# A scan with two feed-forward layers: weights of layer 2 prepared over 30 groups instead of 24, and a scheduler that lets fewer operations compete

## The chip, the cores and the metric

One core of a Trainium2 chip runs the kernel. The metric is the device time of one execution in microseconds (us), the median of several executions. The core has TensorE (PE), which multiplies, VectorE (DVE), ScalarE (ACT) and GpSimd (POOL), which work on elements, and SyncE (SP), from whose queue all transfers of this kernel are issued.

## The reference

```python
S, D, d_ff = 6080, 256, 2048                 # all in float32
sig = 1 / (1 + exp(-f_logit));  f = lower_bound + (1 - lower_bound) * sig
for t in range(S):
    h = f[:, t] * h + (1 - f[:, t]) * x[:, t];  y[:, t] = h       # gated scan
g = y @ w1_in;  y1 = maximum(0.01 * g, g) @ w1_out                # layer 1
g = y1 @ w2_in; out = where(g > 0, g, exp(minimum(g, 0)) - 1) @ w2_out   # layer 2
```

## The kernel before

**Tiles.** The 6080 tokens are cut into 12 chunks: eleven of 512, and chunk 1 of 448. The hidden width of 2048 is cut into four groups `q`, so a layer is 48 groups and the kernel is 96, in the order of a list `stream`: first chunks 0 and 1 by turns, then chunks 2 to 11 of layer 1, then layer 2 from group 48 (`turn2`). The output of layer 1 goes to DRAM (`y1d`, L989) and is fetched again in layer 2 (L605).

**Products.** A float32 product is made of three matmuls in a rounded format (`mm3`): L617 takes the high parts of weight and operand, L618 the low part of the operand, L619 the low part of the weight. So an operand is usable for L617 once ACT has cast its high part (L496 for the scan's rows of chunks 0 and 1, L459 for the sums of later chunks, L797 and L920 for the hidden values), and for L618 once DVE has subtracted (L498, L461, L801, L923). Most products are done with seven multiplications in place of eight, with sums on DVE (L455, L668, L908) and snapshots of a PSUM bank on ACT (L665 into `sn`). L691, L718 and L723 are the activation of layer 1; L728, L732, L738 and L743 on ACT and L734, L740 and L745 on DVE that of layer 2.

**Scan.** `gated` does for each half of the features a tanh and a scaling on ACT (L570, L573), a product on DVE (L577) and the scan (L585); for chunks 0 and 1 PE transposes the inputs (L547), later DVE does (L567).

**Weights.** `weights` makes high and low parts of one unit (`wI0` to `wI7` of the first matrix, `wO0` to `wO3` and `wE0` to `wE3` of the second). A unit is two loads (L337), work on DVE (L365, L374, L378, L392), on POOL (L368) and on ACT (L371, L390). The units of layer 2 also get their sums (L279, ten of the sixteen units) and are stored in DRAM (L399, L401) while layer 1 still uses the weight tiles; `reload` fetches them (L414) when layer 2 begins.

**What sets the order.** Nothing is issued where it stands in the code. Every operation is added to a `Plan` with an engine, a cost, predecessors, buffers that it takes and gives, and a due time. `Plan.emit(near)` (L49) then builds all queues: of the open operations of an engine those that could begin within `near` us of the earliest possible beginning are candidates, and the one with the earliest due time (`rank`) is issued. The costs are the planner's own. Each engine works through its queue in that order; a buffer goes to whoever is issued first.

The sixteen units of layer 2 are called at groups 16, 17, 19, 20, 22, 23, 25, 26, 28, 29, 31, 32, 34, 35, 37 and 38; a unit's due time lies 20 us behind the beginning of its group, and its loads wait for the first product of two groups earlier. `SEVEN` says which groups use seven multiplications for the second matrix as well.

Of the kernel before, what the change touches and what calls it, by code (L numbers as in the profile page):

```python
# [9 lines left out]
F32 = mybir.dt.float32  # L10
# [6 lines left out]
P = 128  # L17
# [95 lines left out]
def kernel(  # L113
# [30 lines left out]
    NQ = NP // 2  # L144
# [10 lines left out]
    NC = len(sizes)  # L155
# [9 lines left out]


    SI, SO = 7 * P, 2 * D
    SEVEN = {1: (1, 2), 2: (0, 1)}

    def sums(l, u):  # L170

        return u[0] == "I" or u[0] == "O" and u[1] in SEVEN[l]

    def stored(u):

        return SO if not sums(2, u) else SI if u[0] == "I" else 8 * P

    units = [("I", z) for z in range(NP)] + [(r, z) for z in range(NQ) for r in "OE"]
    size = {u: SO if u[0] == "E" or u[0] == "O" and not any(u[1] in v for v in SEVEN.values()) else SI for u in units}
    w = {u: const.tile([P, 2 * size[u]], F32R, name=f"w{u[0]}{u[1]}") for u in units}  # L180
    w2d = {u: dram.tile([P, 2 * stored(u)], F32, name=f"w2d{u[0]}{u[1]}") for u in units}
    y1d = [dram.tile([D, n], F32, name=f"y1d{c}") for c, n in enumerate(sizes)]
# [37 lines left out]
    DMA, LATE, FAR, SGN = 0.475, 2.3, 4.5, 0.8  # L220
# [13 lines left out]
    def dma(*a, **k):  # L234
        return plan.add("SP", *a, **k)
# [16 lines left out]

    def seven(l, c, q):

        return q in SEVEN[l] and not (l == 1 and c < 3) and not (l == 2 and c == NC - 1)

    due_in = [0.0]
    for l, c, q in stream:
# [147 lines left out]
    def reload(u, after):  # L406

        q = u[1] // 2 if u[0] == "I" else u[1]
        m = stored(u)

        def load(to, at, n):
            def run():
                dst, src = (t.rearrange("p (j m) -> p j m", j=2) for t in (w[u].bitcast(F32), w2d[u]))
                nc.sync.dma_start(out=dst[:, :, to * P : (to + n) * P], in_=src[:, :, at * P : (at + n) * P])  # L414

            return run

        due = due_in[first[2, "w", q]] + (-12.0 if u[0] == "I" else 0.0)
        parts = [(0, 0, m // P)] if m < 8 * P else [(0, 7, 1), (1, 1, 6)]
        ready = wdone[2, u] + after  # L420
        wdone[2, u] = [dma(2 * part[2] * P / 590.0, due, load(*part), ready, late=LATE) for part in parts]

        def back(after):

            wdone[2, u] = [dma(0.5, due_in[-1 - NQ] - 3.0, load(0, 0, 1), after, late=LATE)]

        return back

# [53 lines left out]
    def rows(c, filled, take, read=()):  # L482

        n = sizes[c]
        xb = {"rows": {}}
        bt = take

        def part(j, k):
            return xb["p"][2][:, 4 * HC * j + k * n : 4 * HC * j + (k + 1) * n]

        last = []
        for k in range(KD):
            def word(k=k):
                return bt["bt"][2][:, k * n : (k + 1) * n]

            hi = act(s1(n), None, lambda k=k, word=word: nc.scalar.copy(out=part(0, k), in_=word()), [filled[k]] + last,  # L496
                     take=[(xb, "p", "op")] if k == 0 else [])
            lo = dve(v1(n), None, lambda k=k, word=word: nc.vector.tensor_tensor(  # L498
                out=part(1, k), in0=word(), in1=part(0, k).bitcast(F32), op=ALU.subtract), [hi])
            last.append(lo)  # L500
            xb["rows"][k] = [lo]
        free([*last, *read], [(bt, "bt", bt["pool"])])
        xb["row"] = lambda k: (part(0, k), part(1, k))
        return xb
# [95 lines left out]
    def fetched(c, gates, hold):  # L600
        n = sizes[c]
        bt = {"pool": "bt"}
        filled = []
        for k in range(KD):
            filled.append(dma(DMA, None, lambda k=k: nc.sync.dma_start(  # L605
                out=bt["bt"][2][:, k * n : (k + 1) * n], in_=y1d[c][k * P : (k + 1) * P, :],
            ), gates + yd[c] + filled[:1], take=[(bt, "bt", "bt")] if k == 0 else [], late=LATE))
        ys[c] = operands(c, filled, bt, (), hold)


# [15 lines left out]
    def group(i):  # L626
# [7 lines left out]
        final = i == len(stream) - 1  # L634
        wi = [o for p in pairs for o in wdone.get((l, ("I", p)), ())]
        wo = {r: wdone.get((l, (r, q)), ()) for r in "OE"}
        if l == 1 and c < 3:
            wo["O"] = wplain.get((l, ("O", q))) or wo["O"]
        count = [0]

# [377 lines left out]

    later = [u for q in range(NQ) for u in (("I", 2 * q), ("I", 2 * q + 1), ("O", q), ("E", q))]
    begin2 = 16  # L1020
    gap = (turn2 - 8 - begin2) / len(later)
    spread = {}
    for z, unit in enumerate(later):
        spread.setdefault(begin2 + int(z * gap), []).append(unit)
# [3 lines left out]
    for i, (l, c, q) in enumerate(stream):  # L1028
        back = [firsts[i - 6] if i >= 6 else None]
        if q == 0:  # L1030
            hold = firsts[i - 1 : i - 1 + 1] if i > 4 else []
            if l == 1:
                gated(c, c < 2, back + ([firsts[i - 4]] if i >= 4 else []), hold)
            else:
                fetched(c, back, hold)
# [6 lines left out]
        if l == 2 and c == 0:  # L1042
            for u in mine:
                backs[u] = reload(u, [last_use[q][u[0] != "I"]])
        if l == 2 and c == NC - 1 and q in SEVEN[2]:
            backs["O", q]([last_use[q][1]])
        at = len(prods)
        o = group(i)
        if l == 1 and c in (1, 2):
            for z in ([q - 1] if q else []) + ([q] if q == NQ - 1 else []):  # L1050
                for u in (("I", 2 * z), ("I", 2 * z + 1)) if c == 1 else (("O", z),):
                    if sums(1, u):
                        finish(u, [prods[-1], outs[-1]])
        firsts.append(prods[at])
        if l == 1 or c == NC - 2:
            last_use[q] = (prods[-1], o)
    plan.emit(0.1)


# [28 lines left out]
```

## Time and profile before

| | |
|---|---|
| median of 3 executions | 994.54 us (994.28 to 1003.21) |
| profiled execution | 995.75 us |
| its span on the core | 993.9 us |
| granted TensorE clock, mean | 0.998 of full speed |
| PE busy | 982.4 us, 99% |
| DVE busy | 878.9 us, 88% |
| ACT busy | 774.5 us, 78% |
| POOL busy | 37.8 us, 4% |

The time of the profiled execution is 1.85 us more than its span, which is what lies around the span. Busy time is counted by instruction; an instruction that waits in front of an engine is not busy. A row of the timeline gives the start, the length, the engine, the line of the kernel, the operation, the tile written and the tiles read, and in brackets the idle time of the engine just before it with what ended it.

### The profile page before, as it was taken

To read this page: it belongs to the slowest core of one execution; us is meant where nothing else is said; L and a number is where in the kernel's file an instruction comes from. 1 tells how busy PE (TensorE), PEld (TensorE's weight loads), DVE (VectorE), ACT (ScalarE), POOL (GpSimd) and SP (SyncE) were. 2 spreads that over 40 slices of the span, in tenths; PEclk is the share of its full clock that TensorE was granted. 3 is DMA by queue.
4 is the path that set the end of the run, shared out by engine and by line. 5 is a ranking of instruction groups with operands and counts; after the bars stand their busy time and mean duration, and the time that the engine had idled before them with its cause. 6 is when DMAs were issued, how large, how long until landed. Compare 5 with 4: busy or idle time off the path is not lost.

```text
span 993.9 us, 20119 instructions
## 1 busy us (share of the span) xinstructions
PE 982.4 (99%) x8234; PEld 969.8 (98%) x8234; DVE 878.9 (88%) x1356; ACT 774.5 (78%) x1139; POOL 37.8 (4%) x38
## 2 busy tenths in 40 slices
PE   7999999999999999999999999999999999999998
PEld 6999999999999999999999999999999999999998
DVE  7899989999999999886678888988988989889875
ACT  6777787887878878867687878788877888788864
POOL 1122000100000010100000000000000000000000
PEclk9999999999999999999999999999999999999999
DMA  6542304435254443302760101101111021010110
GB/s 185 138 115 56 82 12 115 119 97 155 80 150 142 108 138 112 85 23 95 260 226 22 22 22 41 22 23 22 31 35 22 23 44 22 22 23 22 32 22 22
DMA packets 159853, 74.36 MB, mean 75 GB/s; under 512 B 133520, under 2 KB 147600, under 8 KB 159760
## 3 DMA queue, kind: packets, MB, share of 16 engines
q1 hardware_dynamic: 159760, 73.08, 27.4%
q8 instruction: 64, 1.05, 0.4%
q14 instruction: 29, 0.24, 0.1%
HBM read 48.01 MB, written 25.03 MB: 73 GB/s over the span
## 4 chain that ended last, share of the span: by engine, by line
PE 94%; DVE 4%; POOL 1%; issue 1%; DMA 0%; ACT 0%; DVEq 0%; SPq 0%
PE bank L617 28%; PE bank L618 28%; PE bank L619 28%; PE bank L843 2%; PE seed L619 2%; PE seed L618 2%; PE seed L617 2%; POOL ws L368 1%; DVE ws L378 0%; DVE op L801 0%; DVE ws L374 0%; DVE h L279 0%; DVE bt L585 0%; DMA raw<-in_f_logit_dram 0%; DVE up L365 0%
## 5 line engine op out<-in xcount | busy, mean ns | idle before, releaser
L617 PE MATMUL bank<-op,wI 128*128 128x256 f32 (+2 forms) x1136 | 318.1, 280 | 0.8 <-ACT sn L665 0.6
L618 PE MATMUL bank<-op,wI 128*128 128x256 f32 (+2 forms) x1136 | 317.3, 279 | 1.4 <-DVE op L498 1.4
L619 PE MATMUL bank<-op,wI 128*128 128x256 f32 (+2 forms) x1136 | 316.9, 279 | 0.0
L617 PEld LDWEIGHTS bank<-op,wI 128*128 128x128 f32 x1136 | 213.6, 188 | 3.7 <-ACT sn L665 0.9
L618 PEld LDWEIGHTS bank<-op,wI 128*128 128x128 f32 x1136 | 213.5, 188 | 3.6 <-DVE op L498 2.1
L619 PEld LDWEIGHTS bank<-op,wI 128*128 128x128 f32 x1136 | 213.5, 188 | 0.4
L618 PE MATMUL bank<-op,wE 128*128 128x256 f32 (+2 forms) x662 | 190.9, 288 | 0.0
L617 PE MATMUL bank<-op,wE 128*128 128x256 f32 (+2 forms) x662 | 190.8, 288 | 0.0
L619 PE MATMUL bank<-op,wE 128*128 128x256 f32 (+2 forms) x662 | 190.7, 288 | 0.0
L618 PE MATMUL bank<-op,wO 128*128 128x256 f32 (+2 forms) x672 | 187.7, 279 | 0.0
L617 PE MATMUL bank<-op,wO 128*128 128x256 f32 (+2 forms) x672 | 187.7, 279 | 0.0
L619 PE MATMUL bank<-op,wO 128*128 128x256 f32 (+2 forms) x672 | 187.6, 279 | 0.0
L668 DVE TENSOR_TENSOR h<-bank,sn 128x512 f32<-128x512 f32 (+1 forms) x176 | 120.1, 682 | 36.3 <-PE bank L619 30.0
L617 PEld LDWEIGHTS bank<-op,wO 128*128 128x128 f32 x672 | 126.3, 188 | 0.4
L619 PEld LDWEIGHTS bank<-op,wE 128*128 128x128 f32 x662 | 124.3, 188 | 2.3
L619 PEld LDWEIGHTS bank<-op,wO 128*128 128x128 f32 x672 | 126.2, 188 | 0.3
L618 PEld LDWEIGHTS bank<-op,wO 128*128 128x128 f32 x672 | 126.2, 188 | 0.3
L665 ACT COPY sn<-bank 128x512 f32<-128x512 f32 (+1 forms) x176 | 102.6, 583 | 30.0 <-PE bank L619 28.3
L617 PEld LDWEIGHTS bank<-op,wE 128*128 128x128 f32 x662 | 124.5, 188 | 1.3
L618 PEld LDWEIGHTS bank<-op,wE 128*128 128x128 f32 x662 | 124.3, 188 | 1.2
L801 DVE TENSOR_TENSOR op<-h,op 128x1024 fp32r<-128x1024 f32 (+1 forms) x78 | 95.6, 1226 | 8.9 <-ACT op L797 8.4
L801 DVE TENSOR_TENSOR op<-ws,op 128x1024 fp32r<-128x1024 f32 (+1 forms) x72 | 86.1, 1209 | 15.1 <-ACT op L797 15.1
(112 smaller groups left out, 1770.5 us busy)
## 6 DMA issues: line engine op xcount, KB each, us to landing
ws<-in_moe_w_in_dram SPq DMA_DIRECT2D x32, 255.6 KB, 3.7
ws<-in_moe_w_out_dram SPq DMA_DIRECT2D x32, 255.6 KB, 3.3
w2dI<-ws SPq DMA_DIRECT2D x16, 448.0 KB, 3.0
wI<-w2dI SPq DMA_DIRECT2D x8, 896.0 KB, 5.8
y1d<-t SPq DMA_DIRECT2D x22, 256.0 KB, 2.0
bt<-y1d SPq DMA_DIRECT2D x22, 256.0 KB, 2.8
raw<-in_f_logit_dram SPq DMA_DIRECT2D x80, 64.0 KB, 3.0
raw<-in_x_dram SPq DMA_DIRECT2D x80, 64.0 KB, 2.5
```

The source lines that it names most:

```text
L368: sg = pool(SGN, None, lambda: nc.gpsimd.tensor_scalar(out=fr(), in0=top().bitcast(I8), scalar1=2.0, scalar2=-2.0, op0=ALU.min, op1=ALU.ma ...
L617: nc.tensor.matmul(ps[:, s], wop[0], a[0][:, s], start=start and z == 0, stop=False, skip_group_check=True)
L618: nc.tensor.matmul(ps[:, s], wop[0], a[1][:, s], start=False, stop=False, skip_group_check=True)
L619: nc.tensor.matmul(ps[:, s], wop[1], a[0][:, s], start=False, stop=stop, skip_group_check=True)
L665: return act(s1(2 * h), None, lambda: nc.scalar.copy(out=ps(name), in_=ps("X")), after, take=[(b, name, "sn")])
L668: return dve(v1(2 * h), None, lambda: nc.vector.tensor_tensor(out=half(name, s), in0=two(ps(bank)), in1=two(ps(sn)), op=ALU.add), after, **k)
L801: gates[name] = dve(v1(2 * n), None, lambda name=name, g=g: nc.vector.tensor_tensor(out=gate(name, 1), in0=whole(g), in1=gate(name, 0).bit ...
L843: nc.tensor.matmul(dst, ops(part, j, t), wide(z, j), start=s in fresh and t % 2 + j + z == 0, stop=False, skip_group_check=True)
```

## The change

Three things differ that can alter what is issued. The rest of the diff is written otherwise with the same meaning: `SEVEN` becomes a table from layer and group to a range of chunks with the same members, two casts of a type to itself are added, and `hold` and `last_use` are formed otherwise.

1. The stretch over which the units are called ends 2 groups ahead of layer 2 instead of 8. The gap between units is 30/16 = 1.875 groups instead of 24/16 = 1.5, and they are called at groups 16, 17, 19, 21, 23, 25, 27, 29, 31, 32, 34, 36, 38, 40, 42 and 44.
2. `near` is 0.05 us instead of 0.1, for the whole program.
3. The due time of the small reload of `wO1`'s first 128 columns ahead of the last chunk is that of its own group instead of that of the chunk's first group.

```diff
@@ SEVEN
-    SEVEN = {1: (1, 2), 2: (0, 1)}
+    SEVEN = {(1, 1): range(3, 12), (1, 2): range(3, 12), (2, 0): range(0, 11), (2, 1): range(0, 11)}
@@ reload
-        def back(after):
+        def back(i, after):
 
-            wdone[2, u] = [dma(0.5, due_in[-1 - NQ] - 3.0, load(0, 0, 1), after, late=LATE)]
+            wdone[2, u] = [dma(0.5, due_in[i] - 3.0, load(0, 0, 1), after, late=LATE)]
@@ calls
     begin2 = 16
-    gap = (turn2 - 8 - begin2) / len(later)
+    gap = (turn2 - 2 - begin2) / len(later)
...
-            hold = firsts[i - 1 : i - 1 + 1] if i > 4 else []
+            hold = firsts[-1:] if i > 4 else []
...
-        if l == 2 and c == NC - 1 and q in SEVEN[2]:
-            backs["O", q]([last_use[q][1]])
+        if l == 2 and c and c - 1 in SEVEN.get((2, q), ()) and c not in SEVEN[2, q]:
+            backs["O", q](i, [last_use[q][1]])
...
-        if l == 1 or c == NC - 2:
-            last_use[q] = (prods[-1], o)
-    plan.emit(0.1)
+        last_use[q] = (prods[-1], o)
+    plan.emit(0.05)
```

Both programs hold the same instructions on every engine; what differs is their order and which buffer each uses. In three places the order is shown.

At the start, on DVE, from the last two steps of the first weight units to the operands of chunk 1 (`op0`, `op1` are the scan's outputs as operands, `t0` its inputs, `bank3` and `bank5` PE's transposes). Before:

```order
L378 TENSOR_TENSOR ws0_134<-ws0_134 128x512
L392 TENSOR_TENSOR wI0_63<-ws2_136,wI0_63 128x512
L577 SCALAR_TENSOR_TENSOR t0_143<-t2_145,bank3_118 128x512
L392 TENSOR_TENSOR wI1_64<-ws0_134,wI1_64 128x512
L585 SCALAR_TENSOR_TENSOR bt0_129<-t2_145,t0_143 128x512
L365 TENSOR_SCALAR up0_146<-ws1_135 128x512
L498 TENSOR_TENSOR op0_122<-bt0_129,op0_122 128x512
L374 SCALAR_TENSOR_TENSOR ws0_134<-ws1_135,ws0_134 128x512
L577 SCALAR_TENSOR_TENSOR t0_143<-t1_144,bank5_120 128x448
L378 TENSOR_TENSOR ws0_134<-ws0_134 128x512
L585 SCALAR_TENSOR_TENSOR bt0_129<-t1_144,last_h_110,t0_143 128x448
```

And now:

```order
L577 SCALAR_TENSOR_TENSOR t0_143<-t2_145,bank3_118 128x512
L378 TENSOR_TENSOR ws0_134<-ws0_134 128x512
L392 TENSOR_TENSOR wI0_63<-ws2_136,wI0_63 128x512
L585 SCALAR_TENSOR_TENSOR bt0_129<-t2_145,t0_143 128x512
L392 TENSOR_TENSOR wI1_64<-ws0_134,wI1_64 128x512
L498 TENSOR_TENSOR op0_122<-bt0_129,op0_122 128x512
L365 TENSOR_SCALAR up0_146<-ws1_135 128x512
L577 SCALAR_TENSOR_TENSOR t0_143<-t1_144,bank5_120 128x448
L374 SCALAR_TENSOR_TENSOR ws0_134<-ws1_135,ws0_134 128x512
L585 SCALAR_TENSOR_TENSOR bt0_129<-t1_144,last_h_110,t0_143 128x448
L378 TENSOR_TENSOR ws0_134<-ws0_134 128x512
```

The scan's steps L577, L585 and L498 moved ahead of steps of the weights, and L378 of `wO0` moved behind the second scan. On ACT beside it, from the cast of `wO0` to the cast of the first hidden values (`op2`), as a piece of the difference:

```order
+L496 CAST op_123<-bt_129 128x448
+L691 ACTIVATE h_130<-seed_114 128x512
 L390 CAST wO_71<-ws_134 128x512
-L691 ACTIVATE h_130<-seed_114 128x512
-L496 CAST op_123<-bt_129 128x448
+L570 ACTIVATE t_145<-bank_117 128x448
 L797 CAST op_124<-h_130 128x1024
-L570 ACTIVATE t_145<-bank_117 128x448
```

L390 moved behind L496 and L691, and L570 of the next half moved ahead of L797. On ACT some 100 us into the program, at the first products of chunk 2 (`sn1` is the snapshot that frees the bank for the next product), before:

```order
L665 COPY sn0_137<-bank3_118 128x512
L570 ACTIVATE t2_145<-t2_145 128x512
L718 ACTIVATE h0_130<-seed0_114 128x2x256
L573 ACTIVATE t2_145<-t2_145,fb_109,fa_108 128x512
L570 ACTIVATE t0_143<-t0_143 128x512
L665 COPY sn1_138<-bank3_118 128x512
```

And now:

```order
L665 COPY sn0_137<-bank4_119 128x512
L570 ACTIVATE t2_145<-t2_145 128x512
L718 ACTIVATE h0_130<-seed0_114 128x2x256
L573 ACTIVATE t2_145<-t2_145,fb_109,fa_108 128x512
L665 COPY sn1_138<-bank4_119 128x512
L570 ACTIVATE t0_143<-t0_143 128x512
```

The second L665 passed one L570. On DVE in a chunk of layer 2 (the one at 610 us), at the change from one chunk's operands to the next, before:

```order
L801 TENSOR_TENSOR op4_126<-ws2_136,op4_126 128x1024
L461 TENSOR_TENSOR op6_128<-bt0_129,op6_128 128x768
L461 TENSOR_TENSOR op2_124<-bt0_129,op2_124 128x768
L745 SCALAR_TENSOR_TENSOR ws1_135<-ws1_135,h2_132 128x1024
L668 TENSOR_TENSOR h1_131<-bank0_115,sn1_138 128x2x256
L461 TENSOR_TENSOR op2_124<-bt0_129,op2_124 128x256
L801 TENSOR_TENSOR op0_122<-ws1_135,op0_122 128x1024
```

And now:

```order
L801 TENSOR_TENSOR op1_123<-ws1_135,op1_123 128x1024
L461 TENSOR_TENSOR op6_128<-bt0_129,op6_128 128x768
L745 SCALAR_TENSOR_TENSOR ws2_136<-ws2_136,h2_132 128x1024
L461 TENSOR_TENSOR op2_124<-bt0_129,op2_124 128x768
L801 TENSOR_TENSOR op0_122<-ws2_136,op0_122 128x1024
L668 TENSOR_TENSOR h0_130<-bank3_118,sn1_138 128x2x256
L461 TENSOR_TENSOR op2_124<-bt0_129,op2_124 128x256
```

L745 passed the second L461, and L801 of `op0` passed L668. The same move of L745 is made in nine more chunks.

On SP the last unit's two stores (L399, L401 of `w2dE3`) moved from ahead of chunk 9's outputs (L989) to the two refetches of the first chunk of layer 2 (L605): the queue now reads L399, L605, L401, L605, and then the first reload L414 of `wI0`. The small reload of change 3 has kept its place. At the start the load of chunk 1's last inputs (L538) passed one half of a load of weights (L337).

## Rows read from the trace of the kernel before

**Rows 1.** The page: busy time by engine, and the chain that ended last.

```profile
PE 982.4 (99%) x8234; PEld 969.8 (98%) x8234; DVE 878.9 (88%) x1356; ACT 774.5 (78%) x1139; POOL 37.8 (4%) x38
...
PE 94%; DVE 4%; POOL 1%; issue 1%; DMA 0%; ACT 0%; DVEq 0%; SPq 0%
```

**Rows 2.** Waits of PE: waiting line and releaser, total us, times, longest.

```profile
PE bank L618 <- DVE op L498: 1.4, 3, 0.6
PE bank L617 <- ACT sn L665: 0.6, 1, 0.6
PE seed L619 <- DVE wI L392: 0.3, 1, 0.3
PE bank L617 <- ACT op L496: 0.2, 1, 0.2
```

**Rows 3.** Busy time by stretch, with instruction counts, then granted clock, DMA share.

```profile
7.20:10.60 3.40, 1.61 (x12) 1.23 (x10) 3.37 (x5) 0.97 (x2) 0.64 (x2) 1.00 1.01 303
10.60:14.10 3.50, 2.87 (x14) 2.87 (x15) 3.40 (x6) 2.89 (x7) 1.02 (x1) 0.52 0.37 78
...
160.00:400.00 240.00, 240.00 (x2071) 237.99 (x2071) 230.91 (x375) 198.20 (x299) 15.29 (x15) 1.00 0.44 121
400.00:485.00 85.00, 85.00 (x733) 84.19 (x732) 63.91 (x94) 61.34 (x91) 0.55 (x1) 1.00 0.29 94
...
560.00:950.00 390.00, 390.00 (x3325) 386.63 (x3324) 354.58 (x519) 315.60 (x438) 0.00 (x0) 1.00 0.13 27
```

**Rows 4.** Timeline of PE: the late matmuls, and two that are merely longer.

```profile
23.07 0.47 PE L618 MATMUL bank<-op,wI 128*128 128x448 f32 x1 [0.60 <-DVE op L498]
...
28.88 0.47 PE L618 MATMUL bank<-op,wI 128*128 128x448 f32 x1 [0.37 <-DVE op L498]
...
101.24 0.38 PE L617 MATMUL bank<-op,wI 128*128 128x256 f32 x1 [0.55 <-ACT sn L665]
...
212.60 0.38 PE L618 MATMUL bank<-op,wE 128*128 128x256 f32 x1
...
395.18 0.38 PE L617 MATMUL bank<-op,wI 128*128 128x256 f32 x1
```

**Rows 5.** Timeline of DVE: start-up, then the beginning and one chunk of layer 2.

```profile
19.38 0.69 DVE L378 TENSOR_TENSOR ws<-ws 128x512 f32<-128x512 f32 x1
...
22.94 1.21 DVE L801 TENSOR_TENSOR op<-h,op 128x1024 fp32r<-128x1024 f32 x1
...
28.21 0.61 DVE L498 TENSOR_TENSOR op<-bt,op 128x448 fp32r<-128x448 f32 x1
...
491.14 0.95 DVE L461 TENSOR_TENSOR op<-bt,op 128x768 fp32r<-128x768 f32 x1
...
612.88 1.23 DVE L745 SCALAR_TENSOR_TENSOR ws<-ws,h 128x1024 f32<-128x1024 f32 x1
```

**Rows 6.** Timeline of ACT: start-up, and the snapshot at 100 us.

```profile
22.78 0.55 ACT L570 ACTIVATE t<-bank 128x448 f32<-128x448 f32 x1
...
100.09 0.62 ACT L570 ACTIVATE t<-t 128x512 f32<-128x512 f32 x1
100.61 0.57 ACT L665 COPY sn<-bank 128x512 f32<-128x512 f32 x1
```

**Rows 7.** DVE from 160 to 485 us by line: busy us, mean ns, idle before.

```profile
L392 DVE TENSOR_TENSOR ws<-ws,ws 128x896 f32<-128x896 f32 (+2 forms) x16 | 15.2, 952 | 0.9 <-ACT ws L390 0.7
...
L378 DVE TENSOR_TENSOR ws<-ws 128x512 f32<-128x512 f32 x16 | 10.9, 681 | 0.6 <-ACT ws L371 0.2
L374 DVE SCALAR_TENSOR_TENSOR ws<-ws,ws 128x512 int32<-128x512 int32 x16 | 10.8, 672 | 0.0
L279 DVE TENSOR_TENSOR ws<-ws 128x128 f32<-128x128 f32 x40 | 9.8, 283 | 0.1
```

**Rows 8.** Timeline of SP's queue: the last unit's last store, the first refetch.

```profile
409.27 0.34 SPq L401 DMA_DIRECT2D w2dE<-ws  x1
...
456.09 0.88 SPq L605 DMA_DIRECT2D bt<-y1d  x2
```

More of the change, by code (lines that the diff above doesn't have):

```diff
@@ L167 @@
     SI, SO = 7 * P, 2 * D
-    SEVEN = {1: (1, 2), 2: (0, 1)}
+    SEVEN = {(1, 1): range(3, 12), (1, 2): range(3, 12), (2, 0): range(0, 11), (2, 1): range(0, 11)}
     def sums(l, u):
-        return u[0] == "I" or u[0] == "O" and u[1] in SEVEN[l]
+        return u[0] == "I" or u[0] == "O" and len(SEVEN.get((l, u[1]), ())) > 0
     def stored(u):
@@ L178 @@
     units = [("I", z) for z in range(NP)] + [(r, z) for z in range(NQ) for r in "OE"]
-    size = {u: SO if u[0] == "E" or u[0] == "O" and not any(u[1] in v for v in SEVEN.values()) else SI for u in units}
+    size = {u: SO if u[0] == "E" or not (sums(1, u) or sums(2, u)) else SI for u in units}
     w = {u: const.tile([P, 2 * size[u]], F32R, name=f"w{u[0]}{u[1]}") for u in units}
@@ L253, in seven @@
     def seven(l, c, q):
-        return q in SEVEN[l] and not (l == 1 and c < 3) and not (l == 2 and c == NC - 1)
+        return c in SEVEN.get((l, q), ())
     due_in = [0.0]
@@ L605, in fetched @@
             filled.append(dma(DMA, None, lambda k=k: nc.sync.dma_start(
-                out=bt["bt"][2][:, k * n : (k + 1) * n], in_=y1d[c][k * P : (k + 1) * P, :],
-            ), gates + yd[c] + filled[:1], take=[(bt, "bt", "bt")] if k == 0 else [], late=LATE))
+                out=bt["bt"][2].bitcast(F32)[:, k * n : (k + 1) * n], in_=y1d[c][k * P : (k + 1) * P, :],
+            ), gates + yd[c] + filled[:1], take=[(bt, "bt", bt["pool"])] if k == 0 else [], late=LATE))
         ys[c] = operands(c, filled, bt, (), hold)
@@ L636, in group @@
         wo = {r: wdone.get((l, (r, q)), ()) for r in "OE"}
-        if l == 1 and c < 3:
+        if l == 1 and c < min(SEVEN.get((1, q)) or [NC]):
             wo["O"] = wplain.get((l, ("O", q))) or wo["O"]
@@ L1044 @@
                 backs[u] = reload(u, [last_use[q][u[0] != "I"]])
-        if l == 2 and c == NC - 1 and q in SEVEN[2]:
-            backs["O", q]([last_use[q][1]])
+        if l == 2 and c and c - 1 in SEVEN.get((2, q), ()) and c not in SEVEN[2, q]:
+            backs["O", q](i, [last_use[q][1]])
         at = len(prods)
         o = group(i)
-        if l == 1 and c in (1, 2):
+        if l == 1 and c:
             for z in ([q - 1] if q else []) + ([q] if q == NQ - 1 else []):
                 for u in (("I", 2 * z), ("I", 2 * z + 1)) if c == 1 else (("O", z),):
-                    if sums(1, u):
+                    if sums(1, u) and (u[0] == "I" or c == min(SEVEN[1, z]) - 1):
                         finish(u, [prods[-1], outs[-1]])
         firsts.append(prods[at])
-        if l == 1 or c == NC - 2:
-            last_use[q] = (prods[-1], o)
-    plan.emit(0.1)
+        last_use[q] = (prods[-1], o)
+    plan.emit(0.05)
 _INS = ["x", "f_logit", "lower_bound", "moe_w_in", "moe_w_out", "moe2_w_in", "moe2_w_out"]
```

2 lines of the change are left out of this document (1 added, 1 removed).

## The prediction, made before the changed kernel was run

> **What bounds the kernel now.** The first view to read is the page: PE is busy 982.4 us, 99% of the span, and the chain that ended last is PE for 94% [rows 1]. DVE with 88% comes next. So the time is PE's work, which the change leaves alone matmul by matmul, plus the places where PE stands still. Those are the second view, PE's waits [rows 2]. Leaving out the first loads and the identity, which the change doesn't touch, they are 1.4 + 0.6 + 0.3 + 0.2 = 2.5 us in six places, none after 101.24 [rows 4]. The third view, busy time by stretch, says it for the places at which the change is aimed: from 160 to 400 us PE is busy 240.00 of 240.00 us, from 400 to 485 it is 85.00 of 85.00, and from 560 to 950 it is 390.00 of 390 [rows 3]. DVE is nearly full in the first of them, 230.91 of 240 or 96%, has room in the second, 63.91 of 85 or 75%, and 91% in the third. Whatever is moved from the first to the second is moved out from under a PE that didn't wait for it. The reader is to see that a full second engine is not yet a bound: what counts is idle time of PE, and there is next to none.
>
> **The longer stretch.** A unit costs DVE, by its four largest lines, (15.2 + 10.9 + 10.8 + 9.8) / 16 = 2.9 us [rows 7]. At one unit in 1.5 groups of some 10 us that is about 19% of DVE, at one in 1.875 groups about 16%. From 160 to 400 us DVE would so fall from 96% to some 93%, and the share after 400 would rise from 75% by about five units of 2.9 us, 14.5 of 85 us, to some 92%. On PE's path lies of it only what DVE's fullness now costs PE. No wait is counted, but some matmuls last 0.38 us in place of 0.28 since the next one begins late; the first such is at 212.60, the last at 395.18, eight in all [rows 4], and the starts of their successors are together 0.76 us late, an estimate from the timeline's starts at 0.113 us from matmul to matmul. Those are the most that can be gained; a fuller DVE after 400 us could lose as much at the few places where it had its rest. I take -0.4, half of it, with -0.76 and +1.0 as bounds: the emptier engine and the finer order both point down, but the products that ran late are re-ordered too.
>
> **What is moved along with it.** Each unit brings its POOL step, its ACT casts, two loads and two stores. POOL is busy 15.29 of 240 us and 0.55 of 85 [rows 3], so it takes five more steps of about 1 us without queueing. On SP the last store now goes at 409.27 and the first refetch for layer 2 at 456.09 [rows 8]. In the new order one of these refetches stands behind the last unit's second store. The last unit is called six groups later, so that store goes about six times 10.35 us (993.9 / 96) later, at 471 us, and the refetch waits for it: 15 us later than now. Its data are first split by DVE's L461 at 491.14 [rows 5], so some 20 us of cover are left. It costs nothing; if the last unit were still later by more than these 20 us, every us beyond would be a us of PE's. The small reload keeps its place in SP's queue, cost 0, and the load of weights that one load of inputs passes at the start is wanted by an L365 that itself moves back: 0.
>
> **The finer choice, at the start.** Here PE waits in truth. Two of its waits are L618 for L498's low part of chunk 1, 0.60 us ahead of 23.07 and 0.37 ahead of 28.88 [rows 4]. In the new order L577, L585 and L498 go ahead of weight steps, so the first of these waits should go, PE coming some 0.6 us or more earlier to what follows. But that is kept only if the second wait doesn't eat it. The second L498 ends a chain on DVE that begins with L801 of `op2`: from L801's start at 22.94 to L498's at 28.21 are 5.27 us, and L498 lasts 0.61, so that 28.82 releases PE at 28.88 [rows 4, 5]. Between these two the order is the same as before, so the second wait moves with L801's start. L801 needs ACT's L797, and ahead of L797 there stands now one L570 more, 0.55 us [rows 6], and L390 there waits for an L378 (0.69 us, [rows 5]) which has gone behind the second scan. L801 comes between 0 (if the rest of ACT runs that much earlier) and 0.55 + 0.69 = 1.24 us later. I take +0.7, near L570 alone, since ACT has two casts to do before L390. So PE begins again at about 29.6 in place of 28.9: **+0.7**, bounds 0 and +1.2. The earlier gain is lost at this wait: who gets there first only waits longer.
>
> At that second wait PE would stand idle much longer than 0.37 us: the 0.60 us saved, 0.37 and 0.7 make 1.7 us. What such idleness does the start shows: from 7.20 to 10.60 PE was busy 1.61 of 3.40 us at a granted clock of 1.00, and in the 3.50 us after that the granted clock was 0.52, the lower of the two levels, 1.2 instead of 2.4 GHz [rows 3]. By "TensorE: Matmul & The Clock Gate" in the Trainium skill (Part 1, the HAM clock gate), a gate passes half of the clock's pulses after the engine has been idle, and all of them after it has been busy; the rows agree with that, and by this rule the sum would get the price of the second rival on top. I leave it out of the sum, since PE idles at the start now too, and the span's mean clock of 0.998 leaves no room for a second such stretch (the one costs 3.5 x 0.48 / 993.9 = 0.002), and keep it as a rival.
>
> **Two later waits.** L619 waits once for a weight's L392, 0.3 us [rows 2], when the start is over; if PE comes there 0.7 us later, that wait is gone: **-0.25**, bounds -0.3 and +0.5. At 101.24 PE waited 0.55 us for the snapshot L665 [rows 4]. ACT began it at 100.61, directly behind an L570 of 0.62 us [rows 6]; now L665 goes first and can begin at 100.09. It would end 0.52 us earlier: **-0.5**, bounds -0.55 (the whole wait) and +0.2 (where the bank's last product comes later). The scan's L570 and L573 that it passed are due 20 us later on, when that chunk ends.
>
> **Layer 2.** In ten chunks DVE does L745, 1.23 us [rows 5], ahead of the second L461 and so of the next chunk's operand. PE never waits there now, and DVE is idle 390 - 354.58 = 35 us of some ten chunks, 3.5 us in each [rows 3], more than the 1.23 by which the operand comes later; the hidden operand of L801 that passes L668 comes earlier for that. **0**; what it costs if the cover fails is the third rival. The same goes for the end, where PE's order is unchanged.
>
> **The sum.** -0.4 + 0.7 - 0.25 - 0.5 = -0.45 us. The profiled execution took 995.75 us, so it would take 995.3. That execution lies 1.2 us above the median of 994.54, so for the median I take 994.54 - 0.45 = **994.1 us**. About 1%, 10 us, is what a measurement of this kernel can tell from no change; this is far less.
>
> **Rivals.** *One: the order gets rid of nearly every wait.* If the second L618 at the start isn't late either, all 2.5 us of [rows 2] go, of which the 0.2 and the first 0.4 may stay for the weights: -2.1, and with -0.4 for the stretch -2.5: 992.0. For it speaks that DVE's scan steps go first; against it, the chain through ACT's L797 above. *Two, slower: the start loses its wait and the clock.* The mechanism is the one wait at about 29.6 us: +0.7 with nothing given back afterwards is 995.2. If PE's idle time there also brings one stretch at the lower clock, like the 3.50 us from 10.60 on, at most half of that stretch, 1.7 us, is lost: 996.9. [...] *Three, slower: layer 2's new order stalls in each of ten chunks.* If the operand behind L745 is late, PE waits as it does for L498 at the start, 1.4 / 3 = 0.47 us on average [rows 2], or half of that: 10 x 0.23 to 0.47 = +2.3 to +4.7, 996.8 to 999.2. Against it speak the 3.5 us of rest in each chunk. *Four: nothing comes of it,* as the moved work was hidden and the start's terms cancel: 994.5.
>
> **How the numbers follow.** The forecast, 994.1 within about 0.8, gets 0.45; rival one 0.15, two 0.22, three 0.08, four 0.10. The range reaches from rival one's 992.0 to rival two's upper end, 996.9; outside are most of rival three and a tail on either side, with the scatter of some 0.3 us between two executions of the same kernel (994.28 and 994.54). No case that I can price reaches 1% in either direction; 0.01 for faster and 0.02 for slower are left for what I haven't seen.
>
> **What would show it.** In the profile of the changed kernel: PE busy as before, 982 us; in PE's waits one L618 on L498 of over 1 us at about 29.5 us, none at 23; no L665 at 100 us and no L619 on L392; DVE busy some 222 of 240 us from 160 to 400, and over 75 of 85 from 400 to 485, with PE full in both; a granted clock of 1.00 in every stretch after 14 us. The forecast is wrong if that L618 isn't there (one), if a stretch after 28 us has a clock near 0.5 (two), or if L461, L801 or L665 appear among PE's waits once in each chunk of layer 2 (three).

## The result, and the profile after

The changed kernel took 1005.95 us (median of 12 executions, 1002.55 to 1007.35), the kernel before 995.55 us on the same chips (12 executions: eight from 994.28 to 996.50, four from 1001.67 to 1003.78). The ratio of the two is 1.0086 with a 95% interval of 1.0064 to 1.0108; the medians alone would give 1.0104. An execution more than 1.5% above the fastest of its kernel is left out of a ratio. The changed kernel is slower, by 8.6 us by the ratio and by 10.4 us between the medians, and the forecast of 994.1 us (992.0 to 996.9) was wrong. The profiled execution took 1006.94 us, its span is 1005.1 us, 11.2 more than before. The profile of the kernel before, 995.75 us, is one of its shorter executions; no profile here shows a longer one.

The page of the changed kernel, busy time and the chain that ended last, against [rows 1]:

```profile
PE 995.4 (99%) x8234; PEld 983.0 (98%) x8234; DVE 882.6 (88%) x1356; ACT 778.3 (77%) x1139; POOL 35.5 (4%) x38
...
PE 97%; DMA 1%; DVE 1%; ACT 1%; POOL 0%; issue 0%; SPq 0%; DVEq 0%
```

The same 8234 matmuls keep PE busy 13.0 us longer. So the time isn't idle time of PE, and PE's waits of the changed kernel show that too, against [rows 2]:

```profile
PE bank L618 <- DVE op L498: 0.8, 1, 0.8
PE seed L619 <- DVE wI L392: 0.7, 1, 0.7
PE bank L617 <- ACT op L496: 0.4, 1, 0.4
```

That is 1.9 us instead of 2.5. Busy time by stretch, with instruction counts, against [rows 3]:

```profile
160.00:400.00 240.00, 240.00 (x2070) 238.25 (x2070) 225.32 (x362) 196.95 (x294) 11.40 (x12) 1.00 0.40 109
400.00:485.00 85.00, 85.00 (x733) 84.20 (x732) 69.32 (x106) 64.16 (x95) 2.74 (x3) 1.00 0.40 127
560.00:950.00 390.00, 390.00 (x3227) 386.67 (x3225) 348.42 (x507) 308.74 (x427) 0.00 (x0) 1.00 0.13 27
```

The work of the weights has moved: DVE 225.32 us from 160 to 400 (230.91 before) and 69.32 from 400 to 485 (63.91 before). Up to 485 us PE gets as many matmuls done as before. From 560 to 950 us it is just as full, 390.00 us at a granted clock of 1.00, and does 3227 matmuls where it did 3325. To see when that begins, two blocks that both traces have, six matmuls of 512 columns in a chunk of layer 2, are enough. Timeline of PE, first the kernel before, two blocks eight chunks apart:

```profile
598.28 0.40 PE L617 MATMUL bank<-op,wE 128*128 128x512 f32 x1
...
920.52 0.40 PE L617 MATMUL bank<-op,wE 128*128 128x512 f32 x1
```

And the changed kernel:

```profile
598.57 0.40 PE L617 MATMUL bank<-op,wE 128*128 128x512 f32 x1
...
931.17 0.39 PE L617 MATMUL bank<-op,wE 128*128 128x512 f32 x1
```

At 598 us the two differ by 0.29 us, at the later block by 10.65 us. Nearly all of the loss lies in these eight chunks, 40.28 us each before and 41.58 now. What begins there stands in PE's timeline of the changed kernel:

```profile
621.98 0.28 PE L619 MATMUL bank<-op,wE 128*128 128x256 f32 x1
622.09 0.34 PE L617 MATMUL bank<-op,wI 128*128 128x256 f32 x1
622.27 0.28 PE L618 MATMUL bank<-op,wI 128*128 128x256 f32 x1
622.38 0.28 PE L619 MATMUL bank<-op,wI 128*128 128x256 f32 x1
622.50 0.28 PE L617 MATMUL bank<-op,wI 128*128 128x256 f32 x1
622.62 0.28 PE L618 MATMUL bank<-op,wI 128*128 128x256 f32 x1
622.74 0.28 PE L619 MATMUL bank<-op,wI 128*128 128x256 f32 x1
```

One L617 lasts 0.34 us and the next matmul begins 0.06 us late; the waits don't list so short a delay. The reader is to look at what follows: up to there matmuls of 256 columns began every 0.113 us (to the ns, 113, 113 and 114 by turns), from there on every 0.118 (117, 118 and 118). That holds until 975.1 us, in the last chunk, through eight blocks of 512 columns on the way. The load of the late L617's weights had waited for a snapshot; the timeline of ACT there:

```profile
620.46 1.06 ACT L743 ACTIVATE ws<-ws 128x1024 f32<-128x1024 f32 x1
621.42 0.57 ACT L665 COPY sn<-bank 128x512 f32<-128x512 f32 x1
```

L665 ended at 621.99, without a pause behind L743, and PE came 0.06 us too early for it. In the kernel before, the same snapshot and the same product of `wI` stand at nearly the same place of the chunk (timelines of ACT and PE there):

```profile
621.19 0.57 ACT L665 COPY sn<-bank 128x512 f32<-128x512 f32 x1
```

```profile
622.36 0.28 PE L619 MATMUL bank<-op,wE 128*128 128x256 f32 x1
622.48 0.28 PE L617 MATMUL bank<-op,wI 128*128 128x256 f32 x1
```

There the snapshot ended at 621.76, 0.72 us ahead of the product. It is no later now: it begins 0.23 us later in a chunk that lies 0.29 us later. What changed is PE's own queue. Before, PE did twelve matmuls with `wE` ahead of this product; now it does six ahead of it and six behind. Six matmuls are 0.68 us, nearly the whole of the old margin. The orders shown ahead of the prediction are those of DVE, ACT and SP; in layer 2 PE's products were put in another order as well.

I call the two steps, 113.3 and 117.8 ns, PE's fast and slow cadence. The kernel before has both as well: its 7540 steps of 256-column matmuls, stalls left out, hold 700 slow ones (117 ns or more), most of them in stretches of 4 to 25 us; the changed kernel's 7552 hold 3518. The sum of what the steps exceed 113.33 ns by is 3.4 us before and 15.9 after, a difference of 12.5 us. Less the waits, which are 1.0 us shorter with those for the first loads, that is about the 11.2 us of the span.

### The profile page after: what moved, and what is told of

The parts are those of the page before. It is cut to its first block, busy times and chain, and to the rows that moved or that the text cites. A ratio compares the mean times of both kernels' runs of the same rounds, so it can differ in the third digit from the quotient of the medians.

```text
span 1005.1 us, 20100 instructions
## 1 busy us (share of the span) xinstructions
PE 995.4 (99%) x8234; PEld 983.0 (98%) x8234; DVE 882.6 (88%) x1356; ACT 778.3 (77%) x1139; POOL 35.5 (4%) x38
## 4 chain that ended last, share of the span: by engine, by line
PE 97%; DMA 1%; DVE 1%; ACT 1%; POOL 0%; issue 0%; SPq 0%; DVEq 0%
PE bank L619 29%; PE bank L617 29%; PE bank L618 29%; PE bank L843 2%; PE seed L619 2%; PE seed L617 2%; PE seed L618 2%; DMA raw<-in_x_dram 1%; PE bank L547 0%; POOL ws L368 0%; DMA raw<-in_f_logit_dram 0%; DVE ws L378 0%; ACT op L797 0%; DVE ws L374 0%; DVE h L279 0%
## 5 line engine op out<-in xcount | busy, mean ns | idle before, releaser
L617 PE MATMUL bank<-op,wI 128*128 128x256 f32 (+2 forms) x1136 | 319.7, 281 | 0.5 <-ACT op L496 0.4
L618 PE MATMUL bank<-op,wI 128*128 128x256 f32 (+2 forms) x1136 | 319.3, 281 | 0.8 <-DVE op L498 0.8
L618 PEld LDWEIGHTS bank<-op,wI 128*128 128x128 f32 x1136 | 215.3, 190 | 2.6 <-DVE op L498 1.1
L617 PEld LDWEIGHTS bank<-op,wI 128*128 128x128 f32 x1136 | 213.9, 188 | 3.1 <-ACT op L496 0.6
L618 PE MATMUL bank<-op,wE 128*128 128x256 f32 (+2 forms) x662 | 191.9, 290 | 0.0
L617 PE MATMUL bank<-op,wE 128*128 128x256 f32 (+2 forms) x662 | 191.9, 290 | 0.0
L618 PE MATMUL bank<-op,wO 128*128 128x256 f32 (+2 forms) x672 | 189.1, 281 | 0.0
L617 PE MATMUL bank<-op,wO 128*128 128x256 f32 (+2 forms) x672 | 189.0, 281 | 0.0
L668 DVE TENSOR_TENSOR h<-bank,sn 128x512 f32<-128x512 f32 (+1 forms) x176 | 120.2, 683 | 44.0 <-PE bank L619 37.7
L618 PEld LDWEIGHTS bank<-op,wO 128*128 128x128 f32 x672 | 127.3, 189 | 0.5 <-DVE op L801 0.2
L665 ACT COPY sn<-bank 128x512 f32<-128x512 f32 (+1 forms) x176 | 102.3, 582 | 31.9 <-PE bank L619 30.2
L617 PEld LDWEIGHTS bank<-op,wO 128*128 128x128 f32 x672 | 126.2, 188 | 0.4
L618 PEld LDWEIGHTS bank<-op,wE 128*128 128x128 f32 x662 | 125.4, 189 | 1.2
L617 PEld LDWEIGHTS bank<-op,wE 128*128 128x128 f32 x662 | 124.3, 188 | 1.3
L801 DVE TENSOR_TENSOR op<-h,op 128x1024 fp32r<-128x1024 f32 (+1 forms) x78 | 94.7, 1214 | 12.1 <-ACT op L797 11.5
L801 DVE TENSOR_TENSOR op<-ws,op 128x1024 fp32r<-128x1024 f32 (+1 forms) x72 | 86.9, 1211 | 13.2 <-ACT op L797 13.2
```

What stands on the lines that cost most here:

```text
L617: nc.tensor.matmul(ps[:, s], wop[0], a[0][:, s], start=start and z == 0, stop=False, skip_group_check=True)
L618: nc.tensor.matmul(ps[:, s], wop[0], a[1][:, s], start=False, stop=False, skip_group_check=True)
L665: return act(s1(2 * h), None, lambda: nc.scalar.copy(out=ps(name), in_=ps("X")), after, take=[(b, name, "sn")])
L668: return dve(v1(2 * h), None, lambda: nc.vector.tensor_tensor(out=half(name, s), in0=two(ps(bank)), in1=two(ps(sn)), op=ALU.add), after, **k)
L801: gates[name] = dve(v1(2 * n), None, lambda name=name, g=g: nc.vector.tensor_tensor(out=gate(name, 1), in0=whole(g), in1=gate(name, 0).bit ...
```

## The experiments

The **cadence theory**: no engine's added waiting costs the time; the order in layer 2 lets one matmul be 0.06 us late, and PE then goes on in the slow cadence. Its rivals: the **stretch** (longer preparation), the **start or layer 1**, and **placement** (the buffers that the new order picks make each matmul slower).

**The two parts apart.** `e1_near_only` is the kernel before with

```diff
-    plan.emit(0.1)
+    plan.emit(0.05)
```

> The kernel before with emit(0.05) alone; the sixteen units are called over 24 groups as before. The cadence theory (the lost time is no wait: after a late matmul PE can fall from 113.3 to 117.8 ns from matmul to matmul and stay there, and with the finer choice's order of layer 2 nothing brings it back) expects 1002 to 1007 us, with a stretch of hundreds of us at 117.8 ns in layer 2. The stretch theory (the longer preparation costs the time, by what it does to layer 1 and to the buffers at its end) expects 994 to 996.5.

`e2_gap_only` is the changed kernel with `emit(0.1)`.

> The changed kernel with emit(0.1): the units over 30 groups, the choice as before. The cadence theory expects 994 to 996.5 us, slow stretches of PE in layer 2 of at most some 5 us per chunk as in the kernel before. The stretch theory expects 1004 to 1007.

Measured: the finer choice alone 1005.97 us, ratio 1.0110 (1.0095 to 1.0125); the longer stretch alone 994.68, ratio 0.9998 (0.9989 to 1.0007). So the loss is the finer choice's, and the longer stretch alone changes the time by 0.1% at most here (what else it may do stands under the other sizes). Busy time from 660 to 820 us, in the order before, changed, finer choice alone, longer stretch alone:

```profile
660.00:820.00 160.00, 160.00 (x1386) 158.93 (x1385) 146.74 (x216) 129.80 (x180) 0.00 (x0) 1.00 0.13 28
```

```profile
660.00:820.00 160.00, 160.00 (x1337) 158.95 (x1337) 143.63 (x209) 125.78 (x171) 0.00 (x0) 1.00 0.12 26
```

```profile
660.00:820.00 160.00, 160.00 (x1338) 158.95 (x1337) 143.62 (x208) 126.16 (x173) 0.00 (x0) 1.00 0.12 24
```

```profile
660.00:820.00 160.00, 160.00 (x1387) 158.93 (x1386) 146.86 (x216) 129.93 (x181) 0.00 (x0) 1.00 0.13 28
```

The count of matmuls in a stretch in which PE is always busy is a quick way to read the cadence from a profile.

**Where in the program.** `e9_fine_layer1` and `e10_fine_layer2` let the bound depend on the time that the plan has reached, with `turn = due_in[turn2]`:

```diff
-                t, op = min(((t, op) for t, op in starts if t <= first + near), key=lambda p: (p[1].rank, p[1].index))
+                t, op = min(((t, op) for t, op in starts if t <= first + (0.05 if first < turn else 0.1)), key=lambda p: (p[1].rank, p[1].index))
```

and the other way round, 0.1 and then 0.05.

> The changed kernel with 0.05 us only for what the plan begins ahead of layer 2, and 0.1 from there on; start-up, layer 1 and the 30 groups are the changed kernel's, the order in a chunk of layer 2 is that of before. The cadence theory (the order inside layer 2's chunks makes one matmul 0.06 us late some 12 us into a chunk, after which PE stays at 117.8 ns) expects 994 to 997 us, like the kernel before plus up to 0.5 us from the start. If the start or layer 1 cost the time: 1004 to 1007.

> The other way round: 0.1 us ahead of layer 2 and 0.05 from there on. The cadence theory expects 1002 to 1007 us and a slow stretch from about 622 us to the end. If the start or layer 1 cost the time: 994 to 996.

Finer ahead of layer 2 only: 994.40 us, ratio 0.9984 (0.9969 to 0.9999). So neither the start nor layer 1 costs the time, and without its new order in layer 2 the changed kernel has no loss. Finer in layer 2 only: 995.64 us, ratio 1.0019 (0.9985 to 1.0054), with six single executions from 993.79 to 996.43 and three from 1003.06 to 1007.07 (a tenth took 1015.74). Here I had expected the changed kernel's time, and its profiled execution, 994.25 us, has the same late matmul in every one of nine chunks and stays fast. Timeline of PE there, in the chunk that is shown above for the changed kernel:

```profile
621.03 0.28 PE L619 MATMUL bank<-op,wE 128*128 128x256 f32 x1
621.14 0.33 PE L617 MATMUL bank<-op,wI 128*128 128x256 f32 x1
621.31 0.28 PE L618 MATMUL bank<-op,wI 128*128 128x256 f32 x1
621.43 0.29 PE L619 MATMUL bank<-op,wI 128*128 128x256 f32 x1
621.55 0.28 PE L617 MATMUL bank<-op,wI 128*128 128x256 f32 x1
```

Its busy row from 660 to 820 us has 1386 matmuls, like before. To the ns, the step from the late L617 to L618 is 170 or 171 in these nine chunks and 173 in the changed kernel. The late matmul is the same but for these few ns, and PE doesn't fall into the slow cadence. So the order of layer 2 makes the fall possible but doesn't settle whether it comes. The rest of the program doesn't settle it either, as the same program took some 10 us longer in three other executions; of those there is no profile.

**Taking the trigger away.** `e5_after_pad` does three matmuls twice ahead of the second group's first product in each full chunk of layer 2 (the second time starts the bank afresh):

```diff
+                if start and bank == "X" and l == 2 and n == CH and q == 1:
+                    mm3(ps(bank)[:, :h], wop(("I", pairs[0]), s), src["op"](t), True, False)
                 for j, p in enumerate(pairs):
```

> The changed kernel with three matmuls of 256 columns done twice, ahead of the first product of the second group of each of layer 2's eleven full chunks (the real ones then start the bank afresh). The order of everything else is the same; PE comes 0.34 us later to what follows, so it should not arrive ahead of the snapshot L665 at 622 us, where it is 0.06 us late now. Cadence theory with that late matmul as the trigger: PE stays at 113.3 ns from 600 us on, 14 us saved and 11 x 0.34 = 3.7 us added: 994 to 998. If the late matmul is not the trigger: 1006 + 3.7 x 1.04 = 1009 to 1010.

The pad didn't take the late matmul away as I had thought. It changed its step by a few ns: in five chunks from 622 us on the step was 171 and PE stayed fast, 1385 matmuls from 660 to 820 us; in the sixth it was 168 and PE went slow, until 971 us. Timeline of PE of that run at that place, and its busy row for 830 to 930 us (the kernel with finer choice in layer 2 has x865 there):

```profile
825.10 0.28 PE L619 MATMUL bank<-op,wE 128*128 128x256 f32 x1
825.22 0.33 PE L617 MATMUL bank<-op,wI 128*128 128x256 f32 x1
825.38 0.28 PE L618 MATMUL bank<-op,wI 128*128 128x256 f32 x1
```

```profile
830.00:930.00 100.00, 100.00 (x834) 99.21 (x833) 89.70 (x132) 78.72 (x107) 0.00 (x0) 1.00 0.14 28
```

The time, 1009.88 us (1003.11 to 1011.28), ratio 1.0088 (1.0060 to 1.0115), misses the 994 to 998 that I had expected of the cadence theory; it is what I had expected if the late matmul is not the trigger, 1009 to 1010. It doesn't speak against the trigger, as the late matmul was still there. The profiled execution, 1003.11 us and the fastest of ten, shows both outcomes at the same place of one kernel, and its slow stretch begins at the late matmul. But the case that this run was meant to show, the changed order without its late matmul, no run shows.

**Pushing PE by hand.** `e3_after_kick128` puts one matmul of 128 columns ahead of the first product of each group of layer 2's full chunks:

```diff
+                if start and bank == "X" and l == 2 and n == CH:
+                    nc.tensor.matmul(ps(bank)[:, :128], wop(("I", pairs[0]), s)[0], w["I", pairs[0]][:, :128],
+                                     start=True, stop=False, skip_group_check=True)
                 for j, p in enumerate(pairs):
```

`e6_after_kick_q0` does so with `and q == 0` only; `e8_after_kick_wI0` in every group, but always with `wI0`.

> The changed kernel with one more matmul of 128 columns ahead of the first product of each of layer 2's 44 groups of full chunks; it writes into a bank that the product's first matmul then starts afresh, so the result is the same. No wait and no order of another engine is changed. The cadence theory expects that some of these matmuls of another width bring PE back to 113.3 ns, so no slow stretch from 620 us to the end: 44 x 0.06 to 0.11 = 2.6 to 4.8 us are added and 5 to 14 us saved, 994 to 1003. A theory of placement (the buffers that the new order picks make each matmul slower) expects 117.8 ns throughout and 1008 to 1011.

> The changed kernel with one more matmul of 128 columns ahead of the first group of each full chunk of layer 2 only (11 in all). In the run with one in every group those ahead of a chunk's first group always brought PE from 117.8 back to 113.3 ns. Cadence theory: PE is slow from the late matmul some 12 us into a chunk to the next chunk's first group, or not at all: at most 28 of 40 us in each of nine chunks, 1.1 us each, so 996 to 1004, below the changed kernel's 1006. A theory of placement expects 1006 to 1008.

> As the run with 44 matmuls of 128 columns, but all of them with weight and operand from wI0. If what they read decides whether they bring PE back, those of all four groups now bring it back from 117.8 ns (and each fast stretch is lost at the next one): 1000 to 1006. If their place in the chunk decides, only those of first groups do, and the time is that run's 1009 to 1011.

Measured: 1009.81 us, ratio 1.0148 (1.0131 to 1.0165); 1003.07 us, ratio 1.0038 (1.0013 to 1.0062); and 1008.83 us, a single execution. The time of the first is the one that placement expected, but its trace says otherwise: in every chunk from 600 us on PE is slow for three groups and fast for one. When PE was fast, such a matmul put it into the slow cadence each time; when it was slow, those of two groups left it so and that of the third brought it back. I had misread which group that was when I wrote the expectations of the other two runs: it is the third of a chunk, not the first. So the second run does the opposite of what I meant: each of its matmuls from 617 us on makes a fast PE slow, and the block of 512 columns ends that 22 us later, in every chunk but the last. Timeline of PE in that run (L657 is the added matmul, and the starts behind it are 0.12 us apart), and its busy time in the slow and the fast stretch of that chunk:

```profile
617.55 0.28 PE L619 MATMUL bank<-op,wI 128*128 128x256 f32 x1
617.66 0.22 PE L657 MATMUL bank<-wI 128*128 128x128 f32 x1
617.72 0.33 PE L617 MATMUL bank<-op,wI 128*128 128x256 f32 x1
617.89 0.28 PE L618 MATMUL bank<-op,wI 128*128 128x256 f32 x1
618.01 0.28 PE L619 MATMUL bank<-op,wI 128*128 128x256 f32 x1
```

```profile
618.00:641.00 23.00, 23.00 (x194) 22.82 (x193) 22.11 (x35) 17.52 (x24) 0.00 (x0) 1.00 0.13 33
642.00:659.00 17.00, 17.00 (x152) 17.00 (x151) 14.15 (x19) 14.11 (x22) 0.00 (x0) 1.00 0.08 13
```

23 us with 194 matmuls and 17 with 152 are 118.6 and 111.8 ns each, give or take one matmul at the edges. Placement is refuted: buffers and orders of the other engines are the changed kernel's, and one short matmul makes the same products go slow or fast. The third run, with always the same weight, has PE slow and fast in the same groups as the first, so what the added matmul reads doesn't decide.

**What ends a slow stretch.** `e4_before_no512` is the kernel before with

```diff
-            unbroken = (r, j) == ("E", 1) and q < 1
+            unbroken = False
```

> The kernel before without its blocks of six matmuls of 512 columns, one in each chunk (each becomes twelve of 256). In the trace of before every slow stretch of layer 2 ends at such a block. The cadence theory expects slow stretches that then last much longer, hundreds of us: 1000 to 1008. If the blocks have nothing to do with it, 21 blocks x 6 x 6 ns are saved: 994 to 995.5.

1016.26 us, ratio 1.0222 (1.0198 to 1.0245), more than I had expected: without the blocks PE is slow from 277 to 548 us and from 651 to 978. Busy time from 300 to 500 us (before, with the blocks: x1729):

```profile
300.00:500.00 200.00, 200.00 (x1701) 200.00 (x1700) 168.94 (x263) 152.75 (x228) 6.13 (x7) 1.00 0.39 113
```

So in the kernel before it is the blocks that keep a late matmul cheap: the late matmul of its layer 2's chunks, 0.04 us at 755.73 for instance, comes 3.6 us ahead of a block, and the block ends what it begins. In the changed kernel the late matmul comes 17 us ahead, and neither the next block nor the seven behind it end the slow cadence. The distance isn't the reason, as in `e6_after_kick_q0` the blocks end what began 22 us ahead of them. What the traces show is a difference at the block itself: the step of its first matmul is 233 to 236 ns in all 56 blocks that end a slow stretch and 230 or 231 ns in all 22 that leave it (225 or 226 where PE is fast). So it seems to hang on where in its rhythm PE meets the block; no run tests that.

**Other sizes, and a version that is better.** `e11_near_0.2` is the changed kernel with `emit(0.2)`. `e7_before_kick_c2` and `e12_gap_kick_c2` add the matmul of 128 columns with `l == 2 and c == 2 and q == 0`, to the kernel before and to `e2_gap_only`.

> The changed kernel with a coarser choice, 0.2 us, and yet another order in layer 2's chunks. The cadence theory doesn't say which order stumbles, only that the time follows from it: either no late matmul far ahead of a block of 512 columns and 993 to 997, or one and 1000 to 1008, with PE's busy time up by as much as the time. A theory that a finer choice as such is worse expects 994 or less.

> The kernel before with one more matmul of 128 columns, ahead of the first group of layer 2's chunk 2 (at 576 us). In all profiles so far PE goes at 117.8 ns from there to 600 us. Cadence theory: if it ends that stretch, 24 us x 3.8% = 0.9 us less, 993.9 against 994.8; if it doesn't, the same within 0.1. Other theories: the same.

> The units over 30 groups with 0.1 us, and one more matmul of 128 columns ahead of the first group of layer 2's chunk 2, which in the kernel before ended the slow stretch from 576 to 600 us. Cadence theory: 0.9 us less than the run without it, 993.8; if the slow stretches are spread otherwise in each execution, no difference that can be told.

The coarser choice took 1001.80 (the profiled execution), 1006.02 and 1013.94 us, ratio 1.0115 (1.0071 to 1.0159); a fourth, 1016.87, is left out. So finer isn't worse as such. This order has late matmuls in other places and 2115 slow steps. The single matmul did end the stretch from 576 to 600 us in both profiles. On the kernel before the median is 997.47 us and the ratio 0.9984 (0.9958 to 1.0011), not to be told from no change: six executions took 994.10 to 996.22, six 998.72 to 1002.01, and the kernel before beside it splits in the same way (15 of 29 up to 997.15, 14 from 1000.02). With the longer stretch it is 994.39 us, 0.9982 (0.9964 to 1.0000). That and the finer choice ahead of layer 2 alone are the best of this study, 0.2% ahead of the kernel before and just at the edge of what the measurement tells.

Both of these have the longer stretch, and none of their 22 executions took over 996.5 us, where 7 of the 29 of the kernel before beside them took 999.97 to 1002.74. So the longer stretch may keep the longer executions away. `e2_gap_only` can't say so: it had none, but ran where the kernel before had none in 13 either. Whether the longer executions are slow cadence too, no profile shows.

**The sum over the runs.** For each profiled execution I took all steps from one 256-column matmul to the next under 125 ns and summed what they exceed 113.33 ns by. What is left of the span is nearly the same everywhere (the three runs that add 33 matmuls or more are left out):

| kernel | span, us | slow cadence costs, us | rest, us |
|---|---|---|---|
| before | 993.9 | 3.4 | 990.5 |
| changed | 1005.1 | 15.9 | 989.2 |
| e1, finer choice alone | 1004.1 | 14.8 | 989.3 |
| e2, longer stretch alone | 992.1 | 3.3 | 988.8 |
| e4, no blocks of 512 | 1013.5 | 24.2 | 989.3 |
| e6, 11 added matmuls | 1001.4 | 10.9 | 990.5 |
| e7, one added matmul | 992.4 | 2.2 | 990.2 |
| e9, finer ahead of layer 2 | 992.2 | 3.1 | 989.1 |
| e10, finer in layer 2 | 992.1 | 2.9 | 989.2 |
| e11, 0.2 us | 999.7 | 9.7 | 990.0 |
| e12, longer stretch, one added matmul | 992.5 | 2.6 | 989.9 |

Spans differ by 21 us, the rest by 1.7. So it is shown, not only argued, that the time is lost in PE's pace, and the added matmuls show that a single matmul can set that pace. That layer 2's new order is needed for the loss is shown by the finer choice ahead of layer 2 alone, which has none. That it is the late matmul at 622 us which begins the slow stretch is read from the traces, where the stretch begins at it; no run took it away alone.

## Why the prediction was wrong

**The step that failed** is the first: that the time is "PE's work, which the change leaves alone matmul by matmul, plus the places where PE stands still". The work is the same, but its pace isn't a constant: PE was busy 995.4 us, not 982. With it fell the term for layer 2, 0 us, which measured 11.9 us (from 485 us on the slow steps cost 2.5 us before and 14.4 now). Its reason, 3.5 us of rest per chunk on DVE, was right about DVE and looked at the wrong queue: PE's own order had changed, so that PE came 0.06 us ahead of a snapshot that was no later than before, and I had priced such a delay at what it lasts. The third rival had the place, layer 2's new order, and the direction, by another mechanism (a stall in each of ten chunks); its 996.8 to 999.2 us came nearest and is still 6.8 us short. At 0.08 it got too little, and the range left it out. The row that could have warned me stood in the kernel before: the two matmuls "that are merely longer", at 212.60 and 395.18 [rows 4]. I took their lateness as the whole cost and didn't count matmuls in the stretches behind them; behind 395.18 PE was slow for 8 us. The table of before had another warning, the execution of 1003.21 us among three: I took the scatter as 0.3 us from the other two. And the lower end of the range was added up wrong by 0.2 us: 2.5 less 0.2 and 0.4 is 1.9, so rival one gives 992.2.

**The longer stretch**: DVE's shares came out as forecast from 160 to 400 us, 225.32 us against "some 222", and less than forecast from 400 to 485, 69.32 against over 75: 5.4 us more than before are about two units of 2.9 us, where I had five. The gain of 0.4 us can't be told, `e2_gap_only` being 0.9998 (0.9989 to 1.0007). In the changed kernel's trace the late starts from 160 to 485 us did shrink from 0.76 to 0.22 us, but the slow steps there grew from 0.63 to 1.09 and took most of that back. The cover on SP held, as PE had no wait at the layers' border, and was larger than I had put it: the refetch behind the last unit's store went at 457.72, not 471.

**The start**: the step through L797 was right to 0.1 us. L801 began at 23.59 (forecast 23.6) and the second L618 at 29.52 (29.6), and the first wait for L498 is gone. But PE's wait at the second was 0.79 us, not over 1 us: PE got there later than I had it. Timelines of DVE and PE of the changed kernel:

```profile
23.59 1.23 DVE L801 TENSOR_TENSOR op<-h,op 128x1024 fp32r<-128x1024 f32 x1 [0.37 <-ACT op L797]
```

```profile
29.52 0.47 PE L618 MATMUL bank<-op,wI 128*128 128x448 f32 x1 [0.79 <-DVE op L498]
...
80.68 0.39 PE L619 MATMUL seed<-op,wI 128*128 128x256 f32 x1 [0.69 <-DVE wI L392]
```

The granted clock stayed at 1.00 behind it, so the second rival's half-clock stretch didn't come. But my reading of the start was wrong: the clock column shows 1.00 also where the profile has no level on record, and there the starts of the matmuls have to be read. Timeline of PE of the changed kernel:

```profile
15.55 0.41 PE L619 MATMUL bank<-op,wI 128*128 128x256 f32 x1
15.76 0.41 PE L617 MATMUL bank<-op,wI 128*128 128x256 f32 x1
...
16.39 0.28 PE L617 MATMUL bank<-op,wI 128*128 128x256 f32 x1
16.50 0.28 PE L618 MATMUL bank<-op,wI 128*128 128x256 f32 x1
```

Up to 16.3 us matmuls of 256 columns start 0.21 us apart, behind it 0.11: PE ran at the lower level from its first matmuls on and then changed to the upper one for good. In the kernel before, the matmuls of 128 columns up to 7 us start 0.21 us apart too, and those behind 8.6 us 0.11. So the stretch from 10.60 us on was its second at the lower level, and the mean of 0.998, from which I argued that there was room for one only, doesn't count the first. This isn't the change's doing: `e2_gap_only` and `e10_fine_layer2` have the same choice ahead of layer 2, and one is at the upper level from 9 us on, the other from 16.

Of the **two later waits** the snapshot's at 100 us is off the list, as forecast. The one for L392 didn't go but grew from 0.3 to 0.7 us: I had moved PE later there and not DVE, whose L392 began at 79.95 in place of 78.86. Up to the blocks at 598.28 and 598.57 the whole came to +0.3 us, slow stretches of both included, where I had -0.45.

## What to carry to other kernels

When one engine is busy all the time, read from the profile not only its idle time but how many instructions it gets done in equal stretches; a change of order can alter the pace. When a scheduler is changed, compare the queue of the bounding engine itself, not only those that feed it. Between two orders that look alike I would prefer the one in which nothing arrives at the bounding engine within 0.1 us of its need; no run here tests that bound, and a later place where the pace can be set right is no safeguard by itself, as eight blocks in the changed kernel did nothing. And a difference of 1% can come and go between neighbouring orders, and between executions of one order: time several of both before believing in either.

## What was not expected of the hardware

TensorE at a granted clock of 1.00 ran streams of 256-column float32 matmuls, each with its own weight load, at one of two steadily kept paces, 113.3 or 117.8 ns from start to start. It changed from one to the other at a late matmul (0.035 us was enough), at one short matmul, or, from slow to fast only, at a block of 512 columns, and otherwise kept its pace in layer 2's chunks of 512 tokens, for up to 353 us (622.1 to 975.1 in the changed kernel). The 448-column matmuls of the first chunks take 202 ns on average in both kernels. The Trainium skill, "TensorE: Matmul & The Clock Gate" (Part 1, "Wait — 56ns, not 53.3ns?"), gives the step of warm back-to-back matmuls as the columns at 2.4 GHz plus some 2.5 ns, which would be 109.2 ns for 256 columns, an estimate by that page. Neither measured pace agrees with it; here each matmul has a weight load of its own.

What stays open is what the two paces are made of: a collision of the weight loads with the reading of the operands would fit a cost that comes and stays with the phase between them, but no run here tells it from another cause. Open too is what decides, among steps of 168 to 173 ns, which one falls: of those at the place shown, 168 and 173 fell, 170 and 171 never did. At other places it is otherwise: 170 ns behind an added matmul of 128 columns made a fast PE slow each time, and in the kernel before a late matmul with a step of 152 ns fell once and twice didn't.
